# An opening written out stage by stage, constants made by matmuls from one row, and transposes and scaling further ahead: RWKV5 attention with a top-1 expert layer

## The chip, the cores and the metric

The kernel runs on one core of one Trainium2 chip. The metric is the device time of one execution in microseconds (us), smaller is better. Most executions of one kernel agree within about 1%. A run over 1.5% above the fastest of its kernel in the batch counts as slow; the medians below include such runs, the ratios leave them out. The profile is one execution taken by the hardware profiler; its span is some 1.6 us shorter than the time that is reported for the same run. PE is TensorE (matmuls), PEld its weight loads, DVE VectorE, ACT ScalarE, POOL GpSimd, SP SyncE.

## The reference

Four sequences of 768 positions, 8 heads of 48 columns. Each head carries a 48 x 48 state:

```python
for t in range(S):
    cur   = einsum('bhd,bhe->bhde', u * k[t], v[t])      # bonus for the present position
    y[t]  = einsum('bhd,bhde->bhe', r[t], state + cur)
    state = w * state + einsum('bhd,bhe->bhde', k[t], v[t])
# x = y as (4, 768, 384)
e   = argmax(mean_t(x) @ w_gate)          # one of 8 experts for a whole sequence
out = gate_weight * (relu(x @ w1[e]) @ w2[e])
```

## The kernel before

A sequence is cut into three blocks of 256 positions, so there are 12 blocks, called g. For each block: k and r are scaled by powers of the decay w (`prep`), transposed on PE and copied out (`transposes`), multiplied into scores and masked on DVE (`scores`, `gt`), multiplied with v and summed into the running state (`scores_v`), and the bonus is added. After the third block of a sequence a gate picks the expert, whose two weight matrices (768 KB each) are loaded by an address that POOL reads from the gate's result. The expert's work is a list of 28 jobs per sequence; later blocks take them up in "slots", so that PE has work while it waits. In the first sequence there are no jobs yet, and slots hold filler matmuls.

```python
    nc.sync.dma_start(out=wbc, in_=w.rearrange("h d -> (h d)").partition_broadcast(128))
    load(0); load(1)                                        # k, r, v of a block, fp32, 384 KB each
    ...                                                     # four scattered loads of w and u
    nc.scalar.activation(out=lnw, in_=wbc, func=ACT.Ln)     # then dk, dr = Exp(lnw * position)

    def bonus(g):
        y0 = pp_y.tile([128, 512], FP32, tag="y0", name=f"y0_{g}")
        ...
                nc.tensor.matmul(out=y0[:, DM + H * c : DM + H * c + H], ...)   # 16 columns behind y
        nc.vector.tensor_copy(tcol, y0[:, DM : DM + 2 * H])
        nc.gpsimd.tensor_mul(vt, vbs[g]..., tcol...)

    def scores_v(g, j, first):
        ...                                                 # values into y, state into s_ps
        nc.vector.tensor_mul(st, sp[:, 0 : 2 * D * NP]..., mask)   # DVE reads the state's bank

    for g in range(N):                                      # N = 12; one loop from the first block on
        prep(g + 2)
        transposes(g + 1, 0); slot()
        scores_v(g, 1, True); slot()
        transposes(g + 1, 1)
        ...                                                 # outputs of g, scores of g + 1, slots
        if last: gate(b)                                    # index, then softmax weight
        bonus(g + 1); slot()
        if last: weights(b)
```

Of the kernel before, what the change touches and what calls it, by code (L numbers as in the profile page):

```python
# [18 lines left out]
def kernel(  # L19
# [29 lines left out]
    AHEAD = 6  # L49
# [3 lines left out]
    work = ctx.enter_context(tc.tile_pool(name="work", bufs=3))  # L53
# [29 lines left out]
    wbc = const.tile([128, H, D], FP32, tag="wbc", name="wbc")  # L83
    nc.sync.dma_start(out=wbc, in_=w.rearrange("h d -> (h d)").partition_broadcast(128))
    load(0)
    load(1)
    wT = const.tile([128, NP], FP32, tag="wT", name="wT")
    uT = const.tile([128, NP], FP32, tag="uT", name="uT")
    nc.vector.memset(wT, 1.0)
    nc.vector.memset(uT, 0.0)  # L90
    with nc.allow_non_contiguous_dma(reason="decay and bonus by partition, 1.5 KB each"):
        for a in range(2):
            nc.scalar.dma_start(
                out=wT[64 * a : 64 * a + D, :], in_=w.rearrange("(p a) d -> a d p", a=2)[a])
            nc.scalar.dma_start(
                out=uT[64 * a : 64 * a + D, :], in_=u.rearrange("(p a) d -> a d p", a=2)[a])
    wg = const.tile([128, NCT, E], FP32, tag="wg", name="wg")
    nc.scalar.dma_start(out=wg, in_=moe_w_gate.rearrange("(p ct) e -> p ct e", p=128))
# [6 lines left out]

    def fill(cnt, cols):
        for _ in range(cnt):
            t = pp_moe.tile([128, 512], FP32, tag="moe", name="fill")
            nc.tensor.matmul(out=t[:, 0:cols], lhsT=zero[:, 0:128], rhs=zero[:, 0:cols],  # L109
                             start=True, stop=True)  # L110

    fill(24, 512)
# [13 lines left out]
    NR = 3  # L126
# [6 lines left out]

    lnw = const.tile([128, H, D], FP32, tag="lnw", name="lnw")
    nc.scalar.activation(out=lnw, in_=wbc, func=ACT.Ln)
# [23 lines left out]

    U8 = const.tile([128, NP, H], BF16, tag="U8", name="U8")  # L160
    nc.vector.memset(U8, 0.0)
    wcmask = const.tile([128, NP, 2 * D], FP32, tag="wcmask", name="wcmask")
    ones_col = const.tile([128, 1], BF16, tag="ones_col", name="ones_col")
    nc.vector.memset(ones_col, 1.0)

    def late_constants():
        for p in range(NP):
            for a in range(2):
                q = slice(64 * a, 64 * a + 64)
                nc.vector.tensor_scalar_mul(  # L170
                    U8[q, p, 2 * p + a : 2 * p + a + 1], uT[q, p : p + 1], wT[q, p : p + 1])

    def late_constants2():
        lnwT = const.tile([128, NP], FP32, tag="lnwT", name="lnwT")
        nc.scalar.activation(out=lnwT, in_=wT, func=ACT.Ln)
        wcT = const.tile([128, NP], FP32, tag="wcT", name="wcT")
        nc.scalar.activation(out=wcT, in_=lnwT, func=ACT.Exp, scale=float(L))
        nc.vector.tensor_mul(
            wcmask, bmask.rearrange("q p a d -> q p (a d)"), wcT.to_broadcast([128, NP, 2 * D])
        )  # L180


    vbs, krs, gts, vts, ys, sts, xns = {}, {}, {}, {}, {}, {}, {}
    s_ps, xts, carry = {}, {}, {}
# [6 lines left out]
    def prep(g):  # L191
        kg, rg = raw.pop(("k32", g)), raw.pop(("r32", g))
        vb = work.tile([128, 2, H, D], BF16, tag="vb", name=f"vb{g}")
        c0, c1, cc = slice(0, 1), slice(1, 2), slice(0, 2)
        if g == 0:
            for c in (c0, c1):
                scale(nc.vector, kp[g % NR], kg, dk, c)
                scale(nc.vector, rp[g % NR], rg, dr, c)
        else:
            scale(nc.gpsimd, kp[g % NR], kg, dk, cc)  # L200
            scale(nc.gpsimd, rp[g % NR], rg, dr, cc)
        vsrc = raw.pop(("v32", g)).rearrange("q h c d -> q c h d")
        if g < NB:
            nc.scalar.copy(vb, vsrc)
        else:
            nc.gpsimd.tensor_copy(vb, vsrc)
        vbs[g] = vb

    def transposes(g, c):
        twp = pp_tw.tile([128, 2 * NP, 128], BF16, tag="tw", name=f"twp{g}_{c}")  # L210
        for o, src in ((0, kp[g % NR]), (NP, rp[g % NR])):
            for p in range(NP):
                nc.tensor.transpose(  # L213
                    out=twp[:, o + p, :],
                    in_=src[:, c, 2 * p : 2 * p + 2, :].rearrange("s a b -> s (a b)"),
                    identity=ident,
                )
        if c == 0:
            krs[g] = work.tile([128, 2 * NP, 2, 2, 64], BF16, tag="kr", name=f"kr{g}")
            vts[g] = work.tile([128, NP, 2, 2, 64], BF16, tag="prod", name=f"prod{g}")  # L220
        kr, tw = krs[g], twp.rearrange("q o (j i) -> q o j i", j=2)
        nc.scalar.copy(kr[:, 0:NP, :, c, :], tw[:, 0:NP])  # L222
        nc.vector.tensor_copy(kr[:, NP : 2 * NP, :, c, :], tw[:, NP : 2 * NP])  # L223
        nc.vector.tensor_mul(vts[g][:, :, c], tw[:, 0:NP], kr[:, NP : 2 * NP, :, c, :])  # L224

    def scores(g, rnd):
        kr = krs[g]
# [3 lines left out]
        for pp in range(2):  # L231
            p = 2 * rnd + pp
            for cs in range(2):
                for j in range(2):
                    for a in range(2):
                        q = slice(64 * a, 64 * a + D)
                        nc.tensor.matmul(  # L237
                            out=at[64 * j : 64 * j + 64, a, pp, cs, :],
                            lhsT=kr[q, p, j, cs, :],
                            rhs=kr[q, NP + p, j].rearrange("q c i -> q (c i)"),  # L240
                            start=True,
                            stop=True,
                            skip_group_check=True,
                        )
# [6 lines left out]
    def bonus(g):  # L251
        prod = vts[g]
        y0 = pp_y.tile([128, 512], FP32, tag="y0", name=f"y0_{g}")
        y1 = pp_y.tile([128, 512], FP32, tag="y1", name=f"y1_{g}")
        ys[g] = (y0, y1)
        for c in range(2):
            for p in range(NP):
                nc.tensor.matmul(
                    out=y0[:, DM + H * c : DM + H * c + H], lhsT=prod[:, p, c].rearrange("q j i -> q (j i)"),
                    rhs=U8[:, p, :],  # L260
                    start=(c == 0 and p == 0), stop=(p == NP - 1), skip_group_check=True,
                )
        tcol = work.tile([128, 2 * H], FP32, tag="tcol", name=f"tcol{g}")
        nc.vector.tensor_copy(tcol, y0[:, DM : DM + 2 * H])  # L264
# [5 lines left out]
    def inter(g, j):  # L270
        st, kr = sts.pop((g, j)), krs[g]
        yj = ys[g][j]
        for p in range(NP):
            nc.tensor.matmul(
                out=yj[:, 96 * p : 96 * p + 96],
                lhsT=kr[:, NP + p, j].rearrange("q c i -> q (c i)"), rhs=st[:, p, :],
                start=(j == 0 and p == 0), stop=False, skip_group_check=True,
            )
# [10 lines left out]
    def scores_v(g, j, first):  # L289

        gi = g % NB
        gt, vb, yj = gts[g], vbs[g], ys[g][j]
# [56 lines left out]
    def backs(g):  # L349
# [19 lines left out]
        for d in (vbs, krs, gts, vts, ys):  # L369
            d.pop(g, None)  # L370

    gates = {}
# [12 lines left out]
    def gate(b):  # L385
# [12 lines left out]
        nc.vector.max_index(out=idx8, in_max=top8, in_values=lg)  # L398
        negmax = gpool.tile([128, 1], FP32, tag="negmax", name=f"negmax{b}")
# [7 lines left out]
        gates[b] = (idx8, gw)  # L407
# [4 lines left out]
    def weights(b):  # L412
        idx8, gw = gates[b]
# [14 lines left out]
        for si in range(2 * NB):  # L428
            cell = []
            for half in range(2):  # L430
                jobs.append(
                    lambda si=si, half=half, cell=cell: mm2(b, w2, ht, gw, si, half, cell, obs))
# [15 lines left out]
    def mm2(b, w2, ht, gw, si, half, cell, obs):  # L448
# [29 lines left out]
    SLOTS = 7  # L478
    START = NB * SLOTS + 6
    RATE = 8.5 / SLOTS  # L480
    done = [0, 0.0]

    def slot():
        done[0] += 1
        if done[0] > START:
            done[1] += RATE
            c = int(done[1])
            done[1] -= c
            moe(c)
        else:  # L490
            fill(1, 256)
# [3 lines left out]
    transposes(0, 1)  # L495
    prep(1)
    scores(0, 0)
    late_constants()
    scores(0, 1)
    bonus(0)  # L500
    late_constants2()
    for g in range(N):
        b, gi = divmod(g, NB)
        last = gi == NB - 1
        if g + AHEAD < N:
            load(g + AHEAD)
        if g + 2 < N:
            prep(g + 2)
        nxt = g + 1 < N
        if nxt:  # L510
            transposes(g + 1, 0)
        slot()
        scores_v(g, 1, True)
        slot()
        if nxt:
            transposes(g + 1, 1)
        if gi:
            inter(g, 0)
        scores_v(g, 0, gi == 0)
        add_bonus(g)  # L520
        evac_y(g, 0)
        slot()
        inter(g, 1)
        evac_y(g, 1)
        if nxt:
            scores(g + 1, 0)
        slot()
        backs(g)
        if last:
            pool_sum(b)  # L530
        slot()
        if nxt:
            scores(g + 1, 1)
        slot()
        if last:
            gate(b)
        if nxt:
            bonus(g + 1)
        slot()
        if last:  # L540
            weights(b)
# [31 lines left out]
```

## Time and profile before

| | before |
|---|---|
| time, median of 4 runs (range) | 163.75 us (162.27 to 164.45) |
| span of the profiled run | 161.7 us |
| weights of the first expert issued | 43.10 us |
| first expert matmul (hp) | 52.49 us |
| end of the last matmul | 158.2 us |
| PE busy between those two | 103.88 of 105.71 us |

The page's first two parts and the chain of waits are in the prediction. Two more views of the kernel before are wanted. The first is what PE waited for (engine and line, releaser: us in total, times, longest):

```profile
PE hp L437 <- DMA w<-in_moe_w_dram: 5.5, 1, 5.5
PE twp L213 <- DVE prod L224: 5.0, 5, 2.2
PE at L237 <- DVE gt L245: 3.8, 5, 1.3
```

The second is the timeline of the opening (start, duration, engine, line, operation, out<-in, shape; in brackets the idle time before it and what ended it):

```profile
7.83 0.56 DVE L187 TENSOR_TENSOR kp<-k,dk 128x384 bf16<-128x384 f32 x1 [1.60 <-ACT dk L139]
...
14.18 0.64 PE L237 MATMUL at<-kr 48*64 48x128 bf16 x16 [1.13 <-DVE kr L223]
...
19.21 0.22 PE L311 MATMUL y<-vb,gt 64*128 64x48 bf16 x1
```

These three are the first scaling of k, the first scores, the first values of block 0.

### The profile page before, as it was taken

Reading aid. Unit: us, or ns where it says so; the run is one execution under the profiler, and the core shown is the slowest. Engines: PE = TensorE matmul, PEld = TensorE weight load, DVE = VectorE, ACT = ScalarE, POOL = GpSimd, SP = SyncE. Lnnn points to the kernel's source line nnn. Section 1 sums busy time; section 2 is a strip of 40 time slices with the busy share of each in tenths; the row PEclk is TensorE's granted clock in tenths of the full one; section 3 lists DMA queues with packets and bytes.
Section 4 is the critical chain, followed back from the end, with each engine's and each line's share of the span. In section 5 each row is a group of like instructions: output and inputs, shape, how many; then the busy total and the mean of one; then the engine's idle time right before and its main releaser. Section 6 shows DMA issues by size and latency. Waiting matters only on the chain.

```text
span 161.7 us, 4579 instructions
## 1 busy us (share of the span) xinstructions
PE 138.3 (86%) x1955; PEld 98.5 (61%) x1955; DVE 85.9 (53%) x195; ACT 76.9 (48%) x142; POOL 70.1 (43%) x62
## 2 busy tenths in 40 slices
PE   6933897888640999999999899999999899999991
PEld 2413675667530687786667677776677666676560
DVE  6565967678670366586656746775573231212110
ACT  0967742533420256663535557544564652265331
POOL 4026294977699400936949093397003020000000
PEclk9995579999996599999999999999999999999999
DMA  4999999998999999000998000069930029970034
GB/s 50 256 286 284 304 286 308 236 290 218 267 198 215 268 242 264 4 4 5 160 255 256 14 4 4 0 108 202 266 115 4 0 24 207 160 294 0 0 139 155
DMA packets 41604, 25.67 MB, mean 159 GB/s; under 512 B 38768, under 2 KB 39152, under 8 KB 41584
## 3 DMA queue, kind: packets, MB, share of 16 engines
q1 hardware_dynamic: 39456, 19.07, 41.7%
q0 software_dynamic: 1152, 6.29, 21.1%
q8 instruction: 15, 0.25, 0.6%
q10 hardware_dynamic: 976, 0.02, 0.4%
q14 instruction: 5, 0.04, 0.1%
HBM read 26.95 MB, written 4.72 MB: 196 GB/s over the span
## 4 chain that ended last, share of the span: by engine, by line
PE 66%; DMA 12%; DVE 9%; ACT 6%; SPq 3%; issue 2%; POOLq 0%; POOL 0%
PE hp L437 20%; PE op L456 20%; PE twp L213 7%; DMA w<-in_moe_w_dram 6%; PE at L237 4%; PE y L311 4%; DMA k<-in_k_dram 4%; DVE gt L245 3%; DMA r<-in_r_dram 3%; SPq L76 3%; ACT ht L444 2%; ACT kr L222 2%; PE s L319 2%; DVE kr L223 2%; PE y L284 2%
## 5 line engine op out<-in xcount | busy, mean ns | idle before, releaser
L437 PE MATMUL hp<-xt,w 128*128 128x384 bf16 x192 | 42.1, 339 | 7.1 <-DMA w<-in_moe_w_dram 5.5
L266 POOL TENSOR_TENSOR vt<-vb,tcol 128x768 bf16<-128x768 bf16 x12 | 17.9, 1490 | 44.8 <-DVE tcol L264 43.8
L456 PE MATMUL op<-w,ht 128*128 128x384 bf16 x192 | 34.9, 326 | 0.1
L245 DVE TENSOR_TENSOR gt<-at,mask 128x1024 bf16<-128x1024 f32 x24 | 29.3, 1223 | 8.3 <-PE at L237 8.0
L437 PEld LDWEIGHTS <-w 128*128 128x128 bf16 x192 | 25.2, 148 | 13.9 <-DMA w<-in_moe_w_dram 5.6
L444 ACT ACTIVATE ht<-hp 128x384 bf16<-128x384 f32 x48 | 23.6, 492 | 15.3 <-PE hp L437 14.4
L222 ACT COPY kr<-twp 128x512 bf16<-128x512 bf16 x24 | 14.0, 584 | 27.6 <-PE twp L213 27.5
L456 PEld LDWEIGHTS <-ht 128*128 128x128 bf16 x192 | 17.3, 97 | 11.2 <-issue 0.8
L187 POOL TENSOR_TENSOR kp<-k,dk 128x768 bf16<-128x768 f32 x11 | 20.0, 1817 | 8.6 <-ACT kr L222 8.6
L223 DVE COPY kr<-twp 128x512 bf16<-128x512 bf16 x24 | 10.2, 425 | 19.1 <-ACT kr L222 19.0
L187 POOL TENSOR_TENSOR rp<-r,dr 128x768 bf16<-128x768 f32 x11 | 20.0, 1816 | 0.0
L463 ACT ACTIVATE ob<-op,gw 128x384 f32<-128x384 f32 x16 | 9.3, 582 | 20.4 <-PE op L456 19.4
L446 DVE TENSOR_SCALAR ht<-hp 128x384 bf16<-128x384 f32 x16 | 8.9, 556 | 18.7 <-PE hp L437 18.5
L109 PE MATMUL fill<-zero 128*128 128x256 bf16 (+1 forms) x51 | 15.0, 374 | 1.4 <-DVE zero L104 1.4
L311 PEld LDWEIGHTS <-gt 64*128 64x128 bf16 x384 | 11.8, 95 | 4.9 <-issue 4.0
L237 PE MATMUL at<-kr 48*64 48x128 bf16 x384 | 10.5, 229 | 4.9 <-DVE gt L245 3.8
L213 PE MATMUL twp<-ident,kp 128*128 128x128 bf16 x96 | 10.2, 234 | 5.0 <-DVE prod L224 5.0
L311 PE MATMUL y<-vb,gt 64*128 64x48 bf16 x384 | 14.4, 184 | 0.0
L347 ACT CAST xn<-y 128x384 bf16<-128x384 f32 x24 | 11.1, 478 | 6.0 <-PE y L284 3.9
L466 DVE TENSOR_SCALAR ob<-op,gw 128x384 f32<-128x384 f32 x8 | 4.9, 617 | 14.7 <-PE op L456 14.7
L213 PEld LDWEIGHTS <-kp 128*128 128x128 bf16 x96 | 7.3, 103 | 8.2 <-DVE prod L224 4.8
L237 PEld LDWEIGHTS <-kr 48*64 48x64 bf16 x384 | 7.0, 110 | 8.5 <-issue 7.1
(72 smaller groups left out, 169.6 us busy)
## 6 DMA issues: line engine op xcount, KB each, us to landing
w<-in_moe_w_dram POOLq DMA_DIRECT2D x8, 768.0 KB, 10.4
k<-in_k_dram SPq DMA_DIRECT2D x12, 384.0 KB, 5.7
r<-in_r_dram SPq DMA_DIRECT2D x12, 384.0 KB, 5.8
v<-in_v_dram SPq DMA_DIRECT2D x12, 384.0 KB, 5.5
out_dram<-ob SPq DMA_DIRECT2D x11, 384.0 KB, 5.7
out_dram<-ob SPq DMA_DIRECT2D x2, 192.0 KB, 2.1
wbc<-in_w_dram SPq DMA_DIRECT2D x1, 192.0 KB, 4.2
wT<-in_w_dram ACTq DMA_DIRECT2D x2, 0.8 KB, 5.1
```

Of the source, the lines that this page charges most:

```text
L109: nc.tensor.matmul(out=t[:, 0:cols], lhsT=zero[:, 0:128], rhs=zero[:, 0:cols], start=True, stop=True)
L187: eng.tensor_mul(dst[:, cs, :, 0:D].rearrange("q c h d -> q h c d"), src[:, :, cs, :], dec[:, :, cs, :])
L213: nc.tensor.transpose(out=twp[:, o + p, :], in_=src[:, c, 2 * p : 2 * p + 2, :].rearrange("s a b -> s (a b)"), identity=ident,)
L222: nc.scalar.copy(kr[:, 0:NP, :, c, :], tw[:, 0:NP])
L223: nc.vector.tensor_copy(kr[:, NP : 2 * NP, :, c, :], tw[:, NP : 2 * NP])
L237: nc.tensor.matmul(out=at[64 * j : 64 * j + 64, a, pp, cs, :], lhsT=kr[q, p, j, cs, :], rhs=kr[q, NP + p, j].rearrange("q c i -> q (c i)") ...
L245: nc.vector.tensor_mul(gts[g][:, rnd].rearrange("q a p c t -> q (a p) c t"), at.rearrange("q a p c t -> q (a p) c t"), mask.rearrange("q n ...
L266: nc.gpsimd.tensor_mul(vt, vbs[g].rearrange("q c h d -> q (c h) d"), tcol.to_broadcast([128, 2 * H, D]))
L311: nc.tensor.matmul(out=yj[:, D * h : D * h + D], lhsT=gt[q, p // 2, a, p % 2, c, :], rhs=vb[q, c, h, :], start=(first and i == 0), stop=(c ...
L437: nc.tensor.matmul(out=hp[:, 0:SB], lhsT=w1[:, ct, ft::NFT], rhs=xts[b][:, ct, SB * sb : SB * sb + SB], start=(ct == 0), stop=(ct == NCT - 1),
L444: nc.scalar.activation(out=o, in_=hp[:, 0:SB], func=ACT.Relu)
L456: nc.tensor.matmul(out=op[:, 0:DM], lhsT=ht[:, ft, 128 * si : 128 * si + 128], rhs=w2[:, ft, :], start=(ft == 0), stop=(ft == NFT - 1),)
```

## The change

It is meant to shorten the 52 us before the expert work begins. Its parts:

- w and u arrive as one row of 1.5 KB each; 2 + 16 matmuls spread w over the partitions and turn w and u into columns. The end-of-block decay is made by eight squarings on POOL, and the activation table is loaded once.
- The first sequence is written out, stage by stage, with 512-column fillers between. Input loads go four blocks ahead instead of six; transposed and scaled copies are kept for four blocks instead of three.
- In the loop, transposes are two blocks ahead and scaling three. Expert jobs start with block 4 instead of at the end of block 3.
- ACT copies k and r out of the transpose bank together; before, DVE copied r.
- The bonus sums move from columns behind y, in y's bank, to columns behind the running state, in the state's bank.
- The gate's softmax weight is computed later than its index.

```diff
-    AHEAD = 6
+    AHEAD = 4
-    nc.sync.dma_start(out=wbc, in_=w.rearrange("h d -> (h d)").partition_broadcast(128))
+    nc.sync.dma_start(out=wrow[:, :, 0:D], in_=w.rearrange("(o h) d -> o h d", o=1))
+    nc.scalar.dma_start(out=urow[:, :, 0:D], in_=u.rearrange("(o h) d -> o h d", o=1))
-    fill(24, 512)
+    fill(4, 512)
+    nc.tensor.matmul(out=wps[:, 0:DM], lhsT=one, rhs=wrow[:, :, 0:D], ...)
+    for i, row in enumerate((wrow, urow)):
+        for p in range(NP):
+            nc.tensor.matmul(out=wps[:, o : o + 1], lhsT=row[...], rhs=one[:, 0:1], ...)
+    fill(8, 512)
+    nc.scalar.add_instruction(mybir.InstLoadActFuncSet(..., act_func_set_id=6))
+    while 2 ** (len(wpow) - 1) < L:
+        nc.gpsimd.tensor_mul(t, wpow[-1], wpow[-1])
...
     def bonus(g, now=True):
-        y0 = pp_y.tile([128, 512], FP32, tag="y0", name=f"y0_{g}")
+        if g:
+            tc_ps = s_ps[(g - 1) // NB][:, TC : TC + 2 * H]
...
-    for g in range(N):
+    prep(0); transposes(0, 0); transposes(0, 1); fill(4, 512); prep(1); scores(0, 0)
+    ...                                     # blocks 0 to 2 written out
+    transposes(3, 0); gate(0); weights(0); transposes(3, 1); prep_v(3); gate_weight(0)
+    prep(4); ... ; transposes(4, 0); transposes(4, 1); prep(5); prep_v(5)
+    for g in range(NB, N):
+        scores_v(g, 1, True)
+        bonus(g + 1)
+        prep(g + 3); slot()
+        ...
+        transposes(g + 2, 0)
```

## The prediction

> **What bounds the kernel now.** I read the page first (shares, the 40 slices), then the chain of waits that ended last in order of time, then the timeline of each engine up to 64 us, and last the busy time by stretch.
>
> ```profile
> PE 138.3 (86%) x1955; PEld 98.5 (61%) x1955; DVE 85.9 (53%) x195; ACT 76.9 (48%) x142; POOL 70.1 (43%) x62
> PE   6933897888640999999999899999999899999991
> PEclk9995579999996599999999999999999999999999
> ```
>
> One slice is 4.04 us. From the fourteenth slice on PE is full; before that it is not, and the clock row shows two dips to half, near 12 to 22 us and near 50 to 56 us. So there are two programs: an opening (first of four sequences, no expert weights yet) bound by waits, and a body bound by matmuls. The border is in the chain:
>
> ```profile
> 38.76 1.22 DVE gt L245
> ...
> 42.49 0.58 issue
> 43.08 0.03 POOLq L420
> 43.10 9.35 DMA w<-in_moe_w_dram
> 52.45 0.04 issue
> 52.49 1.18 PE hp L437 x3
> ```
>
> The first weight load is issued at 43.1 us and the first expert matmul starts 9.4 us later. Then the stretches (us; busy time of PE, PEld, DVE, ACT, POOL; clock; DMA share; GB/s):
>
> ```profile
> 48.00:50.00 2.00, 0.00 (x0) 0.00 (x0) 0.00 (x0) 0.00 (x0) 2.00 (x2) 0.90 1.06 217
> 50.00:52.00 2.00, 0.00 (x0) 0.00 (x0) 0.00 (x0) 0.00 (x0) 2.00 (x3) 0.50 1.05 215
> 54.00:55.00 1.00, 1.00 (x8) 0.69 (x7) 0.27 (x1) 0.39 (x1) 0.46 (x1) 0.50 1.14 308
> 62.00:72.00 10.00, 10.00 (x170) 8.04 (x169) 6.67 (x12) 6.30 (x14) 5.80 (x4) 1.00 0.24 65
> ```
>
> PE is empty from 47 to 52.5 us, and its first 3.9 us of work (52.5 to 56.4) run at half clock. Only POOL works through that hole, which matters below:
>
> ```profile
> 43.10 0.72 POOL L416 DMA_DIRECT2D w<-in_moe_w_dram  x1
> 43.82 0.54 POOL L420 DMA_DIRECT2D w<-in_moe_w_dram  x1
> 44.37 1.82 POOL L187 TENSOR_TENSOR kp<-k,dk 128x768 bf16<-128x768 f32 x1
> 46.16 1.80 POOL L187 TENSOR_TENSOR rp<-r,dr 128x768 bf16<-128x768 f32 x1
> 47.91 0.81 POOL L206 CAST vb<-v 128x768 bf16<-128x768 f32 x1
> 48.70 1.46 POOL L266 TENSOR_TENSOR vt<-vb,tcol 128x768 bf16<-128x768 bf16 x1
> ```
>
> One block of 256 positions costs POOL 1.8 + 1.8 + 0.8 + 1.5 = 5.9 us. From 52.5 to the last matmul at 158.2 us the body is 105.7 us; by stretches PE idles there about 1.7 us (0.6 in 92 to 101, 0.6 in 126 to 132, 0.45 in 140 to 150). The half clock costs about half of 3.9, 1.95 us. So the work left at the first expert matmul is 105.7 - 1.7 - 1.95 = 102.0 us at full clock, and 3.5 us follow for the last copy and the store.
>
> **What the Trainium skill says.** "TensorE: Matmul & The Clock Gate", Part 1, has the array fall to half rate after about 3.4 us of idling, and need as much busy time to come back. The trace agrees: last matmul end 47.0, half clock from 49.8 us; work from 52.5, full clock from 56.4. The same page, Part 4, says that transposes don't count as busy; the trace fits (clock falls at 12.0 us, 3.4 us after the last filler, though two bursts of transposes lie between). "ScalarE: Activation LUTs", Table sets, says that ln and exp share a set and need one load; before has four loads of 1.28 us in its opening (4.0, 5.9, 14.7, 16.2), since each Ln and Exp brought its own. What ACT_TABLE_LOAD costs, same page, states 1283 ns; the trace shows 1.28 us.
>
> **The change, part by part.** The matmuls of the body are the same ones; 68 instead of 69 of the 112 expert jobs lie inside the loop, the other one in the tail, no gain. What moves is the opening. I walk it with durations of the trace, engine by engine in the order in which the built program issues.
>
> *Constants.* The 192 KB broadcast (4.2 us to landing) and four scattered loads go; w comes as one row and is spread by a matmul. DVE clears two rows of 512 (about 0.53 us each, from 0.38 for 384), two more kp/rp pads, and so reaches the first scaling at about 7.35 us (before 7.83). All four scalings are then limited by DVE alone: 7.35 to 9.55 (before to 10.27, one waited for r). POOL gets ten tiny products and wcmask instead of DVE's eight L170 products (1.86 us between the two score masks): ready for k of block 1 near 10.2, before 11.1.
>
> *Block 0.* Both halves of the transposes have a bank of their own, and ACT copies k and r together (about 1.0 us for 1024 columns, from 0.58 for 512 and 0.80 for 768), so the turn PE, ACT, DVE, DVE, PE disappears. Copies end at 11.0, scores at 11.05 (before 14.18), masks at 12.8 and 14.5 (before 16.1 and 19.1), first use of vb at 15.0 (before 19.2).
>
> *Blocks 1 and 2.* POOL scales k1, r1, k2, r2 by 17.3, then vt0; transposes of block 2 run at 19.5; outputs of block 0 end near 23.6, block 1 near 29.2, block 2 near 32.5. The spacing is about 5.6 us against 6.8 before (carry L300 at 26.2 and 33.0). The transposes of block 3 wait for the bank until 33.3, the gate's matmul follows, its index is out at 36.0 (before 40.5). No vt stands ahead of the weights on POOL now: issue near 36.7 instead of 43.1, 6.4 us earlier.
>
> *What then follows is not the weights.* With 9.4 us as before, less if fewer loads compete (6.7 was the fastest), w1 is there by 46. But by its program order PE must first do block 3 entirely, and ahead of its outputs stand transposes of block 5, "further ahead" than before. Their k and r come from POOL, which waited in order for the gate's index: two issues to 37.9, k4 r4 41.4, vb4 42.2, vt3 43.7, k5 r5 47.25. That is 9.4 us of POOL work. After it PE does transposes 47.7, outputs of block 3 with two evacuations 50.3, scores and second transposes 51.6, the start of block 4 with its bonus 52.5. First expert matmul: near 52.5, as before.
>
> *The sum.* PE has by then done more: 16 transposes (0.9), carry and half the values of block 4 (0.85), a bonus (0.2): about 1.9 us out of the 102.0. The clock should be full, since its longest gap free of true matmuls is about 2.5 us (39.4 to 41.9) instead of 5.5: 1.95 us. Start of the body: 0. Fewer small stalls (two blocks of transposes in hand): about 0.4. Total 4.3 us, which makes 163.1 - 4.3 = 158.8 us.
>
> **Rivals.** (1) *The weights were the only bound.* Then expert matmuls start near 46, and the time is near 152. For it: the 5.5 us wait on that DMA is the longest single wait of PE. Against: the order, in which no expert job stands before block 4, and 9.4 us of POOL. A quicker index would still move POOL with it; each us there is worth one. (2) *Half clock stays or POOL starts later.* If the index is out at 38 or the gaps fall into one bad window, 2 us go: near 161. For: the clock fell at 12 us already with filler about; the walk has some thirty hand-overs, each of which I may have 0.03 us too short. (3) *ACT becomes the body's bound.* It takes 24 x 0.43 = 10 us more (the r half of the copies); ACT was at 77 us. With only two banks for expert sums, a relu behind a 1.0 us copy could stop PE, 0.3 us a block or 2.4 us in all: near 161. Against: the copies lie beside value matmuls, ACT at about 5.6 us of 9.75 a block. (4) *Four input buffers starve POOL.* Against: each is asked for four blocks, some 37 us, ahead; a load lands in 5.7. Worth nothing, or with weights in the way 1 us.
>
> **Range and chances.** The sum has two sure parts (1.9 of advanced work, some of the clock) and an uncertain one, the start of the body, ±1.5 us; with rivals 2 and 3 upward and part of 1 downward I take 155.8 to 161.3. Two per cent is 3.26 us, 159.85. The middle lies 1.05 us below it, at some 1.9 us of spread: 0.70 faster, 0.28 same, 0.02 slower.
>
> **What would show it.** Index of the first gate near 36 us and weight issue near 36.7; POOL without a hole from there to the scaling of block 5 near 47; PE waiting for that scaling (rp, POOL) ahead of a group of transposes, and not for w; first hp near 52.5 at clock 1.0 with transposes of block 5 already behind it; PE full from there. Wrong if hp starts before 50, if hp still waits for w, if the clock row shows a half after 50 us, or if hp or op wait for ACT in the body more than 1 us in all.

## The result, and the profile after

The changed kernel gives the right values and takes 179.63 us (median of 4 runs, 179.25 to 181.05), against 163.75 us for the kernel before on the same chip. The ratio is 1.0999, 95% interval 1.0893 to 1.1106: slower. (Ratios are the mean time of one kernel's fast runs over that of the other's, so not quite the ratio of the medians.)

Where the 17.7 us between the two profiled spans lie:

| part | before | after | difference |
|---|---|---|---|
| until the first expert matmul | 52.49 | 59.83 | +7.3 |
| from there to the end of the last matmul | 105.71 | 115.92 | +10.2 |
| &nbsp;&nbsp;of it PE idle | 1.83 | 10.44 | +8.6 |
| last copy and store | 3.5 | 3.65 | +0.15 |

The profiled run of the changed kernel is the slowest of its four (181.05 us; the others' spans are 177.6 to 178.2), so 1 to 2 us of the 17.7 belong to this run. Both parts of the program are longer, the second more than the first. The page of the changed kernel:

```profile
PE 150.9 (84%) x1978; PEld 105.6 (59%) x1979; DVE 76.1 (42%) x166; ACT 83.3 (46%) x138; POOL 73.1 (41%) x72
...
PE   4998688963779798967999969769899999999991
...
PEclk9999969995558999996999999987999999999999
```

Before, the PE row was full from the fourteenth slice on. Here (a slice is now 4.49 us) it has holes until the slice that ends at 130 us, with two dips of the clock in them. The half clock, which the prediction took away, is still there, but it has moved out of the expert work into the opening, from 41.2 to about 54.8 us (stretch, its length, busy time of PE, PEld, DVE, ACT, POOL, clock, DMA share, GB/s):

```profile
43.00:52.00 9.00, 5.37 (x92) 3.89 (x83) 2.82 (x7) 2.02 (x2) 8.99 (x6) 0.50 0.99 192
```

The first expert matmuls, at 59.83 us, run at full clock.

**The opening.** Timeline of the changed kernel:

```profile
4.34 1.64 PE L117 MATMUL wps<-wrow,one 1*128 1x384 f32 x2
...
7.35 1.84 PE L122 MATMUL wps<-one,urow 1*128 1x1 f32 x8
...
9.12 3.60 PE L110 MATMUL fill<-zero 128*128 128x512 bf16 x8
9.23 0.49 ACT L152 ACTIVATE lnw<-wps 128x384 f32<-128x384 f32 x1 [4.60 <-PE wps L122]
...
10.47 0.56 DVE L204 TENSOR_TENSOR kp<-k,dk 128x384 bf16<-128x384 f32 x1 [0.54 <-ACT dk L157]
...
15.59 0.42 PE L265 MATMUL at<-kr 48*64 48x128 bf16 x16 [0.71 <-ACT kr L251]
...
19.53 0.19 PE L352 MATMUL y<-vb,gt 64*128 64x48 bf16 x1
```

The Ln needs only the first matmuls, the spread row, but it is released by L122, the last of the 16 one-column matmuls into the same bank (16 in 3.4 us). Then eight fillers stand in PE's order ahead of the transposes, until 12.5 us. The first scaling is at 10.47 us where before had 7.83, the scores at 15.59 where before had 14.18, and the first values at 19.53 where before had 19.21. Between the first scaling and the first values the changed kernel is 2.3 us quicker; the 2.6 us by which it starts later have eaten that.

**From the gate to the first expert matmul**, the timeline of POOL and, in the last line, of PE:

```profile
41.73 0.72 POOL L461 DMA_DIRECT2D w<-in_moe_w_dram  x1 [6.05 <-DVE gw L451]
...
43.01 1.82 POOL L204 TENSOR_TENSOR kp<-k,dk 128x768 bf16<-128x768 f32 x1
...
50.51 1.79 POOL L204 TENSOR_TENSOR rp<-r,dr 128x768 bf16<-128x768 f32 x1
...
59.83 0.69 PE L482 MATMUL hp<-xt,w 128*128 128x384 bf16 x3
```

The weights are issued 1.4 us earlier than before and PE no longer waits for them. But POOL stood idle for 6.05 us in front of that issue, held in its order by the gate's index (39.98 us). The line names gw, which ended last before it; at the next gate the issue (78.16 us) comes before gw (81.18), so gw is not what it waits for. Then POOL has 9.3 us of work (43.01 to 52.30), most of it scaling for blocks 4 and 5 that PE needs first.

**The body.** What PE waited for, in the changed kernel:

```profile
PE s L289 <- DVE st L375: 9.8, 10, 1.7
...
PE twp L241 <- POOL kp L204: 1.2, 1, 1.2
PE twp L241 <- POOL rp L204: 1.1, 1, 1.1
```

The largest wait is new: L289 is the bonus, 8 small matmuls, and it waits ten times, once in nearly every block (four times in the opening, 2.9 us, and six in the body, 6.9 us), for the DVE instruction that reads the state. One of the ten in the timeline:

```profile
102.22 0.39 PE L241 MATMUL twp<-ident,rp 128*128 128x128 bf16 x4
...
102.64 1.01 ACT L251 COPY kr<-twp 128x1024 bf16<-128x1024 bf16 x1 [0.41 <-PE twp L241]
...
103.68 0.42 DVE L252 TENSOR_TENSOR prod<-twp,kr 128x512 bf16<-128x512 bf16 x1 [0.36 <-ACT kr L251]
...
104.49 0.55 DVE L375 TENSOR_TENSOR st<-s,bmask 128x384 bf16<-128x384 f32 x1
105.09 0.34 PE L289 MATMUL s<-U,prod 128*128 128x8 bf16 x8 [1.33 <-DVE st L375]
```

The state st is read by DVE from columns 0 to 383 of a bank; the bonus writes columns further back in the same bank, has nothing to do with st's data, and yet waits until DVE has read. DVE reaches st late, since prod (behind ACT's copy) and a relu stand before it in its order. In the program text the bonus comes directly after `scores_v`, and in the trace PE takes its work in that order, so everything behind it stands as well. The Trainium skill, "PSUM — Partial Sum Buffer", section "PSUM bank collisions raise a hardware error", has the rule that I did not apply: guard PSUM by bank, not by address, because two engines in one bank collide even on different columns. The trace agrees with it as far as it can: 9.8 us of waits between disjoint columns of one bank. The bank is also one tile of the program, and no run tells whether the wait was put there for the bank or for the tile.

### The profile page after: what moved, and what is told of

Its sections match the earlier page's. It is cut to its first block, busy times and chain, and to the rows that moved or that the text cites. A ratio compares the mean times of both kernels' runs of the same rounds, so it can differ in the third digit from the quotient of the medians.

```text
span 179.4 us, 4587 instructions
## 1 busy us (share of the span) xinstructions
PE 150.9 (84%) x1978; PEld 105.6 (59%) x1979; DVE 76.1 (42%) x166; ACT 83.3 (46%) x138; POOL 73.1 (41%) x72
## 4 chain that ended last, share of the span: by engine, by line
PE 66%; ACT 14%; DVE 12%; issue 3%; POOL 2%; POOLq 0%; ACTq 0%
PE op L502 17%; PE hp L482 15%; ACT kr L251 7%; PE twp L241 7%; PE fill L110 5%; PE at L265 4%; DVE gt L273 4%; PE y L352 3%; PE xp L401 3%; DVE st L375 3%; PE y L322 2%; ACT ht L489 2%; PE wps L122 2%; DVE prod L252 2%; PE y L312 2%
## 5 line engine op out<-in xcount | busy, mean ns | idle before, releaser
L482 PE MATMUL hp<-xt,w 128*128 128x384 bf16 x192 | 40.4, 331 | 1.0 <-ACT ob L509 0.4
L251 ACT COPY kr<-twp 128x1024 bf16<-128x1024 bf16 x24 | 24.0, 1013 | 33.5 <-PE twp L241 33.4
L502 PE MATMUL op<-w,ht 128*128 128x384 bf16 x192 | 36.3, 338 | 0.1
L304 POOL TENSOR_TENSOR vt<-vb,tcol 128x768 bf16<-128x768 bf16 x12 | 17.7, 1474 | 38.6 <-DVE tcol L296 38.6
L482 PEld LDWEIGHTS <-w 128*128 128x128 bf16 x192 | 25.7, 147 | 7.7 <-issue 4.2
L502 PEld LDWEIGHTS <-ht 128*128 128x128 bf16 x192 | 18.0, 100 | 12.6 <-issue 3.0
L252 DVE TENSOR_TENSOR prod<-twp,kr 128x512 bf16<-128x512 bf16 x24 | 10.2, 425 | 24.7 <-ACT kr L251 24.6
L110 PE MATMUL fill<-zero 128*128 128x256 bf16 (+1 forms) x56 | 16.4, 393 | 3.1 <-DVE zero L101 2.5
L352 PE MATMUL y<-vb,gt 64*128 64x48 bf16 x384 | 15.3, 186 | 0.3 <-DVE gt L273 0.2
L461 POOL DMA_DIRECT2D w<-in_moe_w_dram x4 | 2.5, 625 | 27.7 <-PE hp L482 15.6
L241 PE MATMUL twp<-ident,kp 128*128 128x128 bf16 x96 | 10.9, 245 | 1.8 <-POOL kp L204 1.2
```

Of the source, the lines that this page charges most:

```text
L110: nc.tensor.matmul(out=fills[-1][:, 0:cols], lhsT=zero[:, 0:128], rhs=zero[:, 0:cols], start=True, stop=True)
L241: nc.tensor.transpose(out=twp[:, o + p, :], in_=src[:, c, 2 * p : 2 * p + 2, :].rearrange("s a b -> s (a b)"), identity=ident,)
L251: nc.scalar.copy(kts[g][:, :, :, c, :], tw)
L252: nc.vector.tensor_mul(prods[g][:, :, c], tw[:, 0:NP], rts[g][:, :, :, c, :])
L304: nc.gpsimd.tensor_mul(vt, vbs[g].rearrange("q c h d -> q (c h) d"), tcol.to_broadcast([128, 2 * H, D]))
L352: nc.tensor.matmul(out=yj[:, D * h : D * h + D], lhsT=gt[q, p // 2, a, p % 2, c, :], rhs=vb[q, c, h, :], start=(first and i == 0), stop=(c ...
```

## The experiments

Eighteen kernels ran, all with correct results. "Before" is the kernel before in the same batch. The second column says which of the two kernels each starts from.

| kernel | start | median us (range) | before | ratio (95%) |
|---|---|---|---|---|
| late_bonus | after | 171.67 (170.94 to 173.51) | 163.60 | 1.0493 (1.0407 to 1.0580) |
| bonus_bank | after | 173.43 (173.27 to 175.30) | 163.60 | 1.0674 (1.0574 to 1.0774) |
| split_copy | after | 178.77 (178.03 to 179.53) | 163.60 | 1.0956 (1.0868 to 1.1043) |
| old_const | after | 179.72 (179.38 to 179.90) | 163.60 | 1.1022 (1.0951 to 1.1093) |
| early_jobs | after | 182.31 (181.24 to 183.16) | 164.19 | 1.1177 (1.1053 to 1.1301) |
| late_early | after | 175.45 (175.39 to 175.64) | 164.19 | 1.0759 (1.0663 to 1.0855) |
| late_prep4 | after | 169.45 (168.05 to 170.26) | 164.19 | 1.0405 (1.0304 to 1.0507) |
| late_early_prep4 | after | 176.22 (174.68 to 178.69) | 164.19 | 1.0731 (1.0595 to 1.0867) |
| late_prep4_rate | after | 169.56 (169.27 to 170.26) | 163.19 | 1.0437 (1.0380 to 1.0493) |
| before_gate | before | 162.41 (161.36 to 163.03) | 163.19 | 0.9970 (0.9906 to 1.0033) |
| before_const | before | 164.85 (164.27 to 165.41) | 163.19 | 1.0146 (1.0091 to 1.0201) |
| before_both | before | 164.30 (163.43 to 165.40) | 163.19 | 1.0103 (1.0040 to 1.0166) |
| before_shift | before | 165.05 (163.94 to 166.09) | 163.38 | 1.0145 (1.0086 to 1.0204) |
| before_both_align | before | 161.12 (160.67 to 163.68) | 163.38 | 0.9877 (0.9818 to 0.9936) |
| late_prep4_align | after | 169.54 (168.07 to 171.49) | 163.38 | 1.0374 (1.0306 to 1.0442) |
| after_align | after | 179.55 (177.96 to 181.20) | 163.38 | 1.0990 (1.0912 to 1.1069) |
| before_shift128 | before | 164.52 (162.54 to 165.33) | 164.61 | 0.9996 (0.9930 to 1.0062) |
| before_both_fill | before | 160.31 (158.13 to 163.08) | 164.61 | 0.9695 (0.9628 to 0.9762) |

### Is it the bonus's bank, or ACT's long copy?

My theory for the body: the bonus waits because it shares the state's bank. The rival, number 3 of the prediction: ACT's 1.0 us copy is the bound. `late_bonus` puts the bonus behind two slots of expert work; `bonus_bank` leaves it in its place and gives it, from block 4 on, a bank of its own; `split_copy` halves ACT's copy and leaves the bonus alone.

```diff
 late_bonus
         scores_v(g, 1, True)
-        if n1: bonus(g + 1)
         if n3: prep(g + 3)
         slot(); scores(g + 1, 0); slot()
+        if n1: bonus(g + 1)
 bonus_bank
+        own = g > NB
+        if own: tc_ps = pp_moe.tile([128, 512], FP32, tag="moe", ...)[:, 0 : 2 * H]
 split_copy
-        nc.scalar.copy(kts[g][:, :, :, c, :], tw)
+        nc.scalar.copy(kts[g][:, 0:NP, :, c, :], tw[:, 0:NP])
+        nc.vector.tensor_copy(rts[g][:, :, :, c, :], tw[:, NP : 2 * NP])
```

> The bonus of the next block moves from the head of the block to after the second expert slot; nothing else changes. Theory (PE waits there for the state product, which DVE can only do after the 1.0 us copy and the product of the last transposes): the idle time of PE ahead of the bonus falls from 9.8 us to under 2, the two clock dips of the body (about 82 to 85 and 119 to 122 us) go, time near 170 us (167 to 173) instead of 179.6. Rival (the 1.0 us copy on ACT itself holds up PE, wherever the bonus stands): the wait only moves to another instruction, time within 2% of 179.6.

> The bonus stays where it is, but from block 4 on it writes to an expert bank of its own instead of the bank of the running state. If the shared bank makes the wait (write after the state product's read), PE's wait before the bonus falls from 1.2 to 1.3 us a block to what the product of k and r alone asks, some 0.4 us: about 5 us less in all, near 175 us. If the data alone makes it, PE's wait and the time stay (179.6 within 1%). A third way: the expert jobs lose a bank to it and hp and op wait instead.

> The copy of the transposes is divided again as in the kernel before: k half on ACT, r half on DVE. Theory: the chain from transposes to product is as long either way (0.59 + 0.43 + 0.43 against 1.01 + 0.43 us), so the time stays within 1% of 179.6. Rival (ACT's whole copy is the bound of the body, the third rival of the prediction): 4 us or more less, 175 or below.

`late_bonus` took 8.0 us off, to 171.67. Its wait is nearly gone in PE's list:

```profile
PE s L289 <- DVE st L375: 0.8, 2, 0.5
```

PE idles 4.1 us in its body of 108.4 us, where the changed kernel had 10.4 in 115.9. `bonus_bank`, with the order untouched, took 6.2 us off; some of its bonus matmuls now wait for prod (1.3 us in all), as a wait on data should:

```profile
PE tc L292 <- DVE prod L252: 1.3, 4, 0.6
...
PE s L292 <- DVE st L378: 0.8, 2, 0.5
```

Two different edits remove the same wait and much the same time, and the second leaves the order alone, so sharing the state's bank (or tile, see above) is the cause and not just the place. The two clock dips of the body (0.72 from 80 to 86 us, 0.83 from 116 to 126 us) are at full clock in `late_bonus`, which has one of 0.89 from 100 to 116 us instead. `split_copy` brought 0.9 us and left the wait for st at 10.2 us: rival 3 is refuted as the main cause.

### Are the constants what delays the opening?

`old_const` puts the broadcast and the scattered loads back into the changed kernel; the twelve fillers all stand at its head.

```diff
-    (rows, the 18 matmuls and the 8 fillers behind them)
+    nc.sync.dma_start(out=wbc, in_=w.rearrange("h d -> (h d)").partition_broadcast(128))
+    (four scattered loads of w and u, as before)
```

> The decay row comes by the 192 KB broadcast load again and the two columns by scattered loads; the schedule stays the changed one, the single table load too. Theory: Ln no longer waits for 18 small float matmuls (until 9.2 us), the first scaling starts near 7.8 instead of 10.5 us, POOL's first block scaling near 11.5 instead of 14.6, the index of the first gate and the first expert matmul come about 3 us earlier, time near 176.5. Rival (the opening's end is set by something else, POOL's chain after the gate or the loads): under 1 us.

The first scaling came at 7.29 us instead of 10.47, as expected, and the first scores at 12.94 instead of 15.59. But the next scaling waited for the load of r until 9.14, first values were at 17.6, 1.9 us earlier, the weights' issue and the first expert matmul only 1.1 us earlier, and the median did not move (179.72 against 179.63 us; the two profiled spans, 178.2 and 179.4, do differ by 1.2). A miss. It settles that the constants' matmuls delay the first scaling by 3 us, and that this alone is not what the time hangs on. Part of the gain went to the clock: from 20 to 24 us it was 0.50 here and 1.00 in the changed kernel. The slow load of r was a first sign of the last cause below.

### Does an earlier start of the expert jobs pay?

`early_jobs` lets block 3 take up jobs. `late_early` does so with the late bonus. `late_prep4` has POOL scale block 4 before it waits for the gate's index, in the 6 us in which it stood idle, with the late bonus. `late_early_prep4` has all three, and `late_prep4_rate` the same at a slower rate of jobs.

```diff
 early_jobs, late_early, late_early_prep4, late_prep4_rate
-        if g >= NB: acc[1] = True          # at the end of the loop body
+        acc[1] = True                      # at its head
 late_prep4, late_early_prep4, late_prep4_rate
     scores_v(2, 1, True)
+    prep(4)
     outputs(2, [gap] * 3)
     ...
     gate_weight(0)
-    prep(4)
 late_prep4_rate
-    RATE = 8.5 / 7
+    RATE = 7.5 / 7
```

> The changed kernel, but the expert jobs may start in block 3 instead of after it (8.5 jobs more inside the loop, where fillers stood). Theory (the expert matmuls wait for the order of the program, not for their weights, which were asked for at 41.7 us): the first hp comes at 51 to 52 us instead of 60, with at most 1 us of waiting for w, and time near 175 us (4 to 5 less than 179.6). Rival (weights as bound, as in the kernel before): PE stops for w from 50 us to well after 53, gain under 2 us.

> Late bonus and early jobs together. If the two costs lie in different stages they add: near 167 us (171.7 less 4 to 5). If the early jobs only move the waits, near 171.

> Late bonus, and POOL scales k and r of block 4 before it waits for the gate's index (it stood idle there for 6 us). The prediction's step on trial: POOL's chain after the weight issue (5.3 blocks of work, 10.6 us in the trace) sets the first expert matmul. Then scaling of block 5 ends near 48.7 instead of 52.3, first hp near 55 instead of 58.6, time near 168.2 (171.7 less 3.5). If something else sets it (copies, half clock of PE): under 1 us.

> All three. With the early jobs the first hp stands near the head of block 3 and should now meet its weights, not POOL: hp waits for w until about 51 us; time 164 to 167, at or above the kernel before (163.6).

> The mended changed kernel: late bonus, block 4 scaled ahead of the gate, expert jobs from block 3 on but 7.5 a block instead of 8.5, so that as many as before (67.5 of 112) lie inside the loop and the tail keeps enough of them to cover the last weights. If early jobs lost only because the last weights came uncovered (issue at 149, first hp of the batch 8.2 us later), the wait for w at the end goes, PE waits for w at the head of block 3 alone (about 3 us), and time is 164 to 167 instead of 176.2. If filling block 3 with expert jobs is of no use in itself: 169 or more, as late_prep4 without it.

Three of these five missed in time; `late_prep4_rate` came out on its second branch (169 or more: filling block 3 with expert jobs is of no use in itself), and `late_prep4` within 1.3 us. `early_jobs` began expert work at 50.63 us, 9 us sooner, and ended 2.7 us later. Its timeline near the end:

```profile
149.27 0.59 POOL L461 DMA_DIRECT2D w<-in_moe_w_dram  x1 [15.01 <-PE op L502]
...
157.47 4.72 PE L482 MATMUL hp<-xt,w 128*128 128x384 bf16 x17 [3.37 <-DMA w<-in_moe_w_dram]
```

The weights of the last sequence can only be asked for when its attention is done. Jobs done sooner are not there any more to cover that load, and PE waits 3.4 us for it. Nor is the load asked for sooner: the jobs lengthen block 3, and the last issue comes 1.8 us later than in the changed kernel (147.47). The early jobs also met the half clock, 0.51 from 52 to 56 us. `late_early` and `late_early_prep4` waited for weights 5.5 and 8.7 us in all; `late_prep4_rate` waited 3.8 us at the head of block 3 instead. An earlier start of the body is worth nothing when the jobs that it uses up are wanted later as cover. `late_prep4`, which moves only POOL's scaling, had its first expert matmul at 55.1 us, 3.4 us earlier than `late_bonus`, and took 2.2 us off the median of another batch; by the ratios it is 0.9%, and their intervals overlap. With `late_prep4_rate` and `late_prep4_align`, which are level with it, it is the best that I found on the side of the changed kernel.

### Which parts help the kernel before?

`before_gate` takes only the late softmax weight, and issues the weights straight after the index; `before_const` only the single table load and the constants on POOL, from the old loads; `before_both` has both.

```diff
 before_gate
-        if last: gate(b)
+        if last:
+            gate(b)
+            weights(b)
         bonus(g + 1); slot()
-        if last: weights(b)
+        if last: gate_weight(b)
 before_const
+    nc.scalar.add_instruction(mybir.InstLoadActFuncSet(..., act_func_set_id=6))
-    (eight products of L170 on DVE; Ln, Exp and product for wcmask)
+    (two products and eight squarings and one product on POOL)
```

> One part of the change alone, on the kernel before: the weight load is issued as soon as the gate's index is there, the gate's weight is worked out later. In the changed kernel index to issue takes 1.6 us (40.1 to 41.7), in the kernel before 2.6 us with a bonus product between. Theory (PE waits 5.5 us for just this load): issue 1 us earlier, first hp near 51.5 instead of 52.5, time 1 us less. Rival: the load meets more of the input loads then and lands no earlier, 0.

> On the kernel before: one table load for Ln and Exp instead of four, the bonus matrix and the state decay by products on POOL, which is idle then, instead of eight products on DVE between the two score masks. The broadcast load stays, no matmul makes a constant. Theory: second mask at 16.1 instead of 17.9 us, so 1.5 to 2 us off the opening, as issue of the weights near 41.5, time 161.5 to 162.5. Rival (POOL's scaling of block 1 is pushed back by its new work, or half clock eats it): within 0.5 us of before.

> Both on the kernel before: the gains lie on one path and should add, 2.5 to 3 us, near 161 us.

`before_gate`: the first expert matmul came at 50.8 us and PE's wait for weights fell from 5.5 to 1.5 us, but the time only to a ratio of 0.997, which its interval does not tell from 1. `before_const` and `before_both` missed: slower by 1.5% and 1.0%, although they take work away. Their loads landed later (first use of r of block 0 at 9.19 instead of 8.77 us, of v of block 2 at 19.51 instead of 17.68). Comparing all runs, I found that each kernel with new constants loads its inputs at about 260 GB/s where before and `before_gate` reach 285 to 320.

### Where the loads lost a tenth

New constants mean new tiles, and those stand ahead of the input tiles in each partition. In the built programs the input tiles start at a multiple of 256 bytes in before and `before_gate`, 192 bytes past one in `before_const` and `before_both`, and 160 past one in the changed kernel. A load writes pieces of 384 bytes. The Trainium skill, "DMA: Bandwidth & Descriptors", section "How a descriptor splits into AXI transactions", says that transactions begin on boundaries of 256 bytes. (It says so of what a transaction reads; that the written side, which these tiles are, follows the same count is my inference.) By that count, pieces that begin 0 and 128 past a boundary in turn need two transactions each; with 192, or 160, every second piece needs three, so 2.5 in the mean. The rival was the table load or the constants themselves. (The count in the expectation of `before_shift128` is by the same section.) The edits are one line, an unused tail on a small constant tile, of 192, 128, 64 or 96 bytes; it shifts all tiles behind it, the weights' and outputs' too:

```diff
-    ones_col = const.tile([128, 1], BF16, tag="ones_col", name="ones_col")
+    ones_col = const.tile([128, 97], BF16, tag="ones_col", name="ones_col")[:, 0:1]
```

> The kernel before with one unused stretch of 192 bytes per partition put ahead of the input tiles, so that they start 192 bytes past a multiple of 256 as in before_const; no instruction differs. If the address is what slows the loads: 260 GB/s from 8 to 20 us (before has 285 to 296), w issue near 44.0, first expert matmul near 53.3, time 164.5 (ratio 1.005 to 1.015). If the single table load or the constants on POOL are what slows them: the rate stays at 285 or more, w issue 43.1, time 163.3, ratio 1.00.

> As before_shift, but moved by 128 bytes instead of 192. A piece of a load is 384 bytes, so pieces start alternately 0 and 128 bytes past a multiple of 256 whether the tile starts at 0 or at 128: each piece is two transactions. With 192 every second piece needs three. If the count of transactions sets the rate: 285 GB/s or more from 8 to 20 us and 163.3, ratio 1.00. If a tile must itself start on a multiple of 256: 260 GB/s and 164.5 to 165.

> before_both with the input tiles moved by 64 bytes to a multiple of 256, nothing else. If the address slows the loads: 290 GB/s or more from 8 to 20 us (before_both had 260), first expert matmul near 51 instead of 53.1, time 161.5 to 162.5, level with before_gate or below it. If something else does: 260 GB/s, 164.3 as before_both.

> late_prep4 with the input tiles moved by 96 bytes to a multiple of 256. If the address slows the loads: 285 GB/s or more from 8 to 20 us (260 before), first expert matmul near 54 instead of 55.1, time near 168.3 instead of 169.5. If it does not matter: 169.5.

> The changed kernel with the input tiles moved by 96 bytes to a multiple of 256. If the address slows the loads: 285 GB/s or more from 8 to 20 us, first values of block 0 near 19 instead of 19.5, first expert matmul near 58.8 instead of 59.8, time near 178.5. The opening still waits for constants and the body is as it was, so most of the loss stays. If it does not matter: 179.6.

Busy times by stretch, 8 to 14 us (stretch, its length, busy time of PE, PEld, DVE, ACT, POOL, clock, DMA share, GB/s). Before:

```profile
8.00:14.00 6.00, 2.27 (x19) 1.44 (x18) 3.04 (x7) 3.40 (x7) 2.88 (x2) 0.84 1.07 285
```

`before_shift`, in which no instruction differs from before:

```profile
8.00:14.00 6.00, 2.66 (x21) 1.70 (x20) 2.82 (x6) 2.75 (x6) 1.84 (x2) 0.90 1.22 258
```

`before_shift128`:

```profile
8.00:14.00 6.00, 2.52 (x30) 1.42 (x31) 3.58 (x8) 4.09 (x8) 2.94 (x2) 0.88 1.10 297
```

The changed kernel:

```profile
8.00:14.00 6.00, 6.00 (x29) 3.78 (x30) 2.25 (x6) 3.01 (x6) 3.23 (x11) 1.00 1.28 260
```

`after_align`:

```profile
8.00:14.00 6.00, 6.00 (x28) 3.78 (x29) 2.25 (x6) 3.02 (x6) 3.23 (x11) 1.00 1.17 323
```

192 bytes cost 1.45% of the whole time, the same as the 1.46% of `before_const`; 128 bytes cost nothing. So a tile need not itself start on a multiple of 256 bytes, as the count of 256-byte boundaries has it. That a piece must begin on a multiple of 128 bytes would fit all these runs as well; none separates the two. The last pair gives the size: 323 / 260 = 1.24, beside the 2.5 / 2 = 1.25 that the count of transactions gives as an estimate by that page. (The page's count of beats would give 30 / 28 = 1.07 here, and 32 / 28 = 1.14 for 192 bytes; 160 and 192 bytes load at the same 258 to 261 GB/s, so the measurement speaks for transactions.) The pair of `before` gives less, 285 / 258 = 1.10. Put back in place, `before_both_align` went from 1.0103 to 0.9877, first expert matmul at 49.17 us. That is 0.9% below `before_gate` of another batch, with intervals that overlap: the constants on POOL probably help once their tiles do no harm, but no run shows it clear of noise.

For the changed kernel it was a miss: loads by a quarter faster, time 179.55 us. Its first values come at 19.53 us with either rate, so they do not wait for loads. In `late_prep4_align` too the time stayed. Its profiled run issued the weights at 42.99 us, later than `late_prep4` (41.69), and had a clock of 0.72 from 24 to 36 us (0.86 there). But that run is one of low clock (mean 0.945, 170.33 us) and the other one of high (0.969, 168.05 us); the fastest run of `late_prep4_align` had 0.969 and 168.07 us. What decides between the two is open.

### What does the half clock at the start of the body cost?

`before_both_align` has first expert work at 49.17 us, but still at half clock. `before_both_fill` adds three empty matmuls in each of two gaps of 1.4 us after the first gate.

```diff
         scores_v(g, 1, True)
+        if g == NB: fill(3, 512)
...
         scores_v(g, 0, gi == 0)
+        if g == NB: fill(3, 512)
         add_bonus(g)
```

> before_both_align with six empty matmuls of 512 columns in the two gaps of 1.4 us in which TensorE waits just after the first gate. If those gaps are what halves the clock from 44 to 53 us: clock near 1.0 there, the first expert matmuls at 49.2 run at full speed, about 1.2 us less, 160.0. If the weights bound that stretch, or the clock falls anyway: 161.1, no change.

Busy times from 43 to 52 us of `before_both_align` (columns as above):

```profile
43.00:52.00 9.00, 7.07 (x80) 4.84 (x79) 4.49 (x8) 2.47 (x5) 8.02 (x6) 0.55 1.05 214
```

And of `before_both_fill`:

```profile
43.00:52.00 9.00, 5.67 (x101) 3.97 (x101) 4.78 (x9) 2.68 (x5) 8.90 (x7) 0.94 0.94 195
```

The clock rose from 0.55 to 0.94, and the time to 160.31 us, near the 160.0 expected. The first expert matmul did not come sooner (49.50): part of what the clock gave became a wait for the weights, 2.3 us instead of 0.5. After that wait the clock fell all the same, to 0.50 from 51 to 54 us, so the fillers shortened the half clock and did not end it. Against the kernel before of its own batch it is 3.05% faster, the only kernel here that beats it by more than 2%. That ratio is flattering: three of its six runs count as slow, being over 1.5% above its fastest, and are left out. (Its profiled run, 160.57 us, is one of the three; its mean clock of 0.957 is not below the 0.956 of two fast ones.) Median over median of all runs is 160.31 / 164.61, 2.6%. It is also another chip than that of `before_both_align`, so the share of the fillers stays uncertain: 0.8 us by the two medians, 1.8% by the two ratios.

## Why the prediction was wrong

The prediction was 158.8 us (155.8 to 161.3), 70% for faster; the result was 179.63 us. By its own steps:

1. **Constants, "reaches the first scaling at about 7.35 us".** Failed: 10.47. I costed DVE's clearing of the rows and took the matmuls of one row as free. The 16 one-column matmuls take 0.21 us each, and Ln waits for all of them; they write the same tile, in one bank, as the row that it reads. Eight fillers hold the transposes until 12.5 us on top.
2. **Block 0, "first use of vb at 15.0".** Failed, in part as a consequence: 19.53, 4.5 us late. With the old constants (`old_const`) it was 17.62, so 1.9 of them came back. The other 2.6 were not taken apart; in `old_const` 1.3 us of waiting for the load of r are among them.
3. **Blocks 1 and 2.** Held: 21.0 us were given from the first values to the gate's index, measured 20.5 (19.5 to 40.0), with 5.5 us between blocks (carry at 27.9 and 33.4) where 5.6 were given. The walk was right from a wrong start. From index to issue it took 1.75 us instead of 0.7.
4. **"What then follows is not the weights".** The mechanism held: PE waits for POOL's kp and rp ahead of transposes and not for the weights (the two listed waits are for block 4, not for block 5 as forecast), `late_prep4`, in which rp of block 5 ends 2.5 us sooner than in `late_bonus` (49.8 instead of 52.3), has its first expert matmul 3.4 us sooner, and POOL's work from the issue to the end of rp of block 5 took 10.6 us, as given (36.7 to 47.25). With the 4.0 us of the late index, 1.05 of the slow issue, and 2.3 more from there to the first expert matmul, a stretch at half clock until about 54.8 us, the start is 7.3 us later than the "0" of the sum.
5. **"The clock should be full: 1.95 us".** Held for the first expert matmuls (1.00 from 58 to 60 us), failed around them: the half clock moved into the opening (41.2 to 54.8 us), and the body got two dips, worth up to 3.4 us by an estimate from their means. I asked only for the longest gap. In the changed kernel the clock fell after 4 us in which PE was busy 2.8, 0.9 of it transposes, with no gap over 0.7 us (1.1 with the transposes left out). In `before_both_align` it fell at 44.0 us, after 4 us in which PE was busy 1.7. The share of busy time alone does not explain it: `before_both_fill` was busy 2.7 of the 4 us from 40 to 44 and kept its clock. The prediction's reading of the kernel before was off too: its clock fell at 49.6 us, not 49.8, 2.6 us after the last matmul, which is shorter than the 3.4 us that it was said to agree with.
6. **"Fewer small stalls: 0.4 us", and "PE full from there".** The biggest failure, by sign and size. The body idles 8.6 us more, and the list of waits has 6.9 us of it at the bonus alone (9.8 with the opening). The move of the bonus to the state's bank was in the diff, and I counted its matmuls and not the wait. `late_bonus` and `bonus_bank` show it to be worth 8.0 and 6.2 us.
7. **"About 1.9 us of work ahead".** Not confirmed. 43 fewer matmuls lie in the body (1301 instead of 1344), but the body of `late_prep4`, at full clock, has 103.05 us of PE busy time, and before's 103.88 contains 1.95 of half clock by my own estimate, so there is no gain left to see: 101.9 us before, 1.1 less.
8. **Rivals.** Number 2 (half clock stays, POOL later) came true in its second half (index at 40.0, not 38) and larger than its 2 us. Number 3 (ACT) was refuted as the main cause. Number 4 (four buffers) looked at how far ahead loads are asked for, and not at their rate, which fell by a tenth to a fifth from the tiles' place. The cause that decided was among none of the four.

What stays open: `late_prep4`, without the two large faults, is still 4% slower than before. 2.6 us of that is its start (55.1 us instead of 52.5) and 2.7 us more idle time in its body (4.5 us instead of 1.8). I did not take this apart, and the address does not explain it, since `late_prep4_align` is no faster.

## What to carry to other kernels

Before you put a result into free columns of a bank, ask who reads the other columns, and when: here the write waited for that reader, and everything behind it in PE's order waited too. When work is moved ahead, ask what it was covering where it stood; expert jobs done early left the last weight load bare. And when a kernel that does less is slower, compare the rate of its loads: a few bytes of constants ahead of the load targets cost 1.5% here, and a tail of 64 bytes more than gave it back.

## What the Trainium skill lacked or had wrong

- "TensorE: Matmul & The Clock Gate", Part 1: its rule is some 3.4 us of idling; a subsection (A second HAM failure mode) has short idles between groups do the same, but gives no share of busy time. Here the clock halved after 4 us in which PE was busy 1.7, with no gap over 1.4 us, or 1.9 with transposes left out (`before_both_align`, 40 to 44 us), and in the changed kernel after 4 us in which it was busy 2.8; filling two gaps of 1.4 us kept it full until 50.9 us. In the kernel before it fell 2.6 us after the last matmul.
- The same page, Back-to-back issue gap: it has small matmuls at about 60 ns or less, and nothing on fp32 ones that each bring their own weights. Sixteen of one column took 3.4 us, 0.21 us each.
- "DMA: Bandwidth & Descriptors", How a descriptor splits into AXI transactions: it gives no rates. Here 2.5 instead of 2 transactions for each 384-byte piece gave 260 instead of 323 GB/s; its beat counts would give 1.07 and not the measured 1.24. Nor does it say that a constant tile elsewhere can shift a load's target, worth 1.45% of this kernel's time.
- "PSUM — Partial Sum Buffer", PSUM bank collisions raise a hardware error: the rule is there, its price is not. Here 9.8 us of waits in ten blocks between disjoint columns.
- "GPSIMD Engine Reference", 2.1 Instruction dispatch: no time for a tiny product is given. Seven squarings of 128 x 4 took 2.55 us, 0.36 us each.
